# Twelve expert-layer blocks of 500 or 502 tokens in place of fourteen of 376 or 470, cut independently of the inverse transform's groups

## The chip, the cores and the metric

The kernel runs on one core of a Trainium2 chip. The metric is device time in microseconds (us); a lower time is better. Engines are called PE (TensorE), ACT (ScalarE), DVE (VectorE), POOL (GpSimd) and SP (SyncE, which issues the DMAs here).

## The reference

Three layers follow one another on 6016 tokens (2 sequences of 3008) of 256 channels:

```
X = rfft(x, axis=1)                      # float64 inside
Yr = Xr @ w_r - Xi @ w_i + b_r           # Yi likewise, with Xr @ w_i + Xi @ w_r + b_i
Y = soft_threshold(Y, 0.01)              # of real and imaginary part
x = irfft(Y, n=3008)
h = x @ w_in;  x = (h * cos(h)) @ w_out                    # first expert layer, 256 -> 2048 -> 256
h = x @ w_in2; out = (h * clip(h + 3, 0, 6) / 6) @ w_out2  # second expert layer
```

The weights of the expert layers come as float64. The kernel splits each operand of a product into a high and a low part of 12 significant bits, and a product is three matmuls (high by high, high by low, low by high).

## The kernel before, in words

**The transform.** The 3008 positions of a sequence are 64 interleaved rows of 47; two neighbouring rows make a pair, so there are 32 pairs a sequence and 94 tokens a pair. For each sequence a first stage (`a_part`, L322 to L337) takes the input in chunks of `A_CHUNKS` pairs: two of PE's float32 matmul instructions for each pair and each half of the channels into `zp`, then ACT copies the high part and DVE makes the low part. `load_x` fetches a chunk's table and input; `XB` chunks are loaded ahead, and each further one is issued after a chunk has been used. A second stage (`k2_step`, twelve a sequence) does the rest of the transform, the linear layer and the threshold in matmuls of 512 columns, and stores the result to DRAM (`u_dram`). The last products of the second stage of sequence 0 (`pend`) are done between the chunks of sequence 1's first stage.

**The inverse transform.** `load_u` (L270) reads a token block's `u_dram` back, and `y_part` (L278) makes one half of its channels with two PE instructions of 94 columns a pair. ACT and DVE split the result straight into the token tiles `tok`, of which a token set is handed out per block.

**The expert layers.** A sequence is cut into seven blocks of `BLOCK_PAIRS` = 5, 5, 5, 5, 4, 4, 4 pairs, that is, 470 or 376 tokens. A unit is one block by 128 of the 2048 hidden channels: six matmuls into a PSUM bank `h` (`mm_h`, L576), the nonlinearity on ACT and DVE (L587 to L611), the split into `gh` and `gl` (L619, L620), and, `DELAY` = 4 units later, six matmuls into two accumulators (`mm_out`, L633). The columns of each matmul are the tokens of the block, at most 512 of them. The order on PE, ACT and SP is written out by hand; DVE and POOL are ordered by the scheduler. The first layer runs `LEAD` blocks ahead of the second: first its blocks alone, then a unit of each layer in turn, and at the end blocks of the second layer alone. Four `h` banks are shared by all stages.

**The weights' conversion.** Float64 words become high and low parts in 32 chunks, 16 for each layer, in a fixed order. A chunk has five steps: clamp, shift, top, exponent, rest on DVE (L151 to L163), with a magnitude on ACT (L148) before and, after the rest, a sum on POOL (L164), the high part on ACT (L167) and the low part on POOL (L170). The high and low part of a chunk are emitted with the third and fourth step of the next chunk. Steps are spread over the program by `RATE_A` (one for each chunk of the first stage from `CV0` on), `RATE_W` (five for each two of the first ten steps of the second stage) and `RATE_M` (five for each four units). Before a product that needs a chunk, `require` emits what is still missing of it at once. `raw` holds the loaded words.

Of the kernel before, what the change touches and what calls it, by code (L numbers as in the profile page):

```python
# [19 lines left out]
# sequence 3008 = 47 * 64:  n = 64*n1 + n2,  k = k2 + 47*j,  n2 = 2*i + s  # L20
# [9 lines left out]
BLOCK_PAIRS = [5, 5, 5, 5, 4, 4, 4]  # L30
A_CHUNKS = [2] + [3] * 10
NFC = DFF // 128
LEAD = 4  # token blocks by which the first expert layer is ahead of the second
DELAY = 4  # units between a product with w_in and the product with w_out that takes it up
WARM = 9
IL, IM = 4, 1  # units after which the jobs of the first and of the later groups take turns
# steps of the weights' conversion in the unit's two places, in the transform, in the linear layer
# [3 lines left out]
LATE, CC, CV0 = [1, 4, 6], 7, 10  # L41
XB = 5
EG, PW = 0, 10
YP, YE = (0, 3, 6), (5, 2)


def _split(a):
    """float64 -> two float32 arrays of 12 significant bits each."""

    def rnd(v):  # L50
        b = v.astype(np.float32).view(np.uint32).astype(np.uint64)
        b = (b + 0x7FF + ((b >> 12) & 1)) & 0xFFFFF000
        return b.astype(np.uint32).view(np.float32)

    hi = rnd(a)
    return hi, rnd(a - hi.astype(np.float64))


def _trig(num, den):
    """cos, sin of 2*pi*num/den with exact zeros and ones."""  # L60
# [50 lines left out]
def fourier_moe_moe_kernel(ctx, tc, x, w_r, w_i, b_r, b_i, ta, tg, fg, win1, wout1, win2, wout2, out):  # L111
# [12 lines left out]
    # ---------------------------------------------------------------- weights  # L124
# [8 lines left out]
    def convert(src, dst_hi, dst_lo, name):  # L133
        """float64 words -> hi + lo, each of 12 significant bits; the instructions in stages"""
        raw = persist.tile([128, 512, 2], I32, tag="raw", bufs=3, name=f"raw{name}")
# [38 lines left out]
    class Converter:  # L174
        """Runs the conversions one VectorE instruction at a time, each chunk's end in the next one's course."""
# [71 lines left out]
    # ----------------------------------------------------------- token blocks  # L247
    blocks = []
    for b in range(NB):
        p0 = 0  # L250
        for n in BLOCK_PAIRS:
            blocks.append((b, p0, n))
            p0 += n
    NBLK = len(blocks)
    MAXP = max(BLOCK_PAIRS)
    MAXT = MAXP * TP

    def tok0(j):
        b, p0, n = blocks[j]
        return b * NSEQ + p0 * TP, n * TP  # L260
# [3 lines left out]
    # token blocks between the parts, transposed, as hi + lo: handed out and taken back in program order  # L264
# [3 lines left out]
    free_sets = [token_set(persist, i) for i in range(2)]  # L268

    def load_u(j):  # L270
        b, p0, n = blocks[j]
        ut = persist.tile([ROWS, MAXP, D], F32, tag="u_sb", name=f"u_sb{j}")
        sp.dma_start(ut[:, :n], u_dram[b][:, :, p0 : p0 + n, :].rearrange("s f i e -> (s f) i e"))
        tt = persist.tile([ROWS, MAXT], F32, tag="tg_sb", name=f"tg_sb{j}")
        sp.dma_start(tt[:, : n * TP], tg[:, p0 * TP : (p0 + n) * TP])
        u_sb[j], tg_sb[j] = ut, tt

    def y_part(j, ec):  # L278
        """inverse transform over k2 for one half of the channels of a token block"""
        b, p0, n = blocks[j]  # L280
        if ec == 0:
            y_sb[j] = free_sets.pop(0)
        yp = psum.tile([128, 512], F32, tag="h", bufs=4, name=f"yp{j}_{ec}")
        for i in range(n):
            pe.matmul(  # L285
                yp[:, i * TP : (i + 1) * TP],
                lhsT=u_sb[j][:, i, ec * 128 : (ec + 1) * 128],
                rhs=tg_sb[j][:, i * TP : (i + 1) * TP],
                start=True,
                stop=True,  # L290
            )
        yh, yl = y_sb[j][ec]
        t = n * TP
        act.activation(yh[:, :t], yp[:, :t], AF.Copy)
        dve.tensor_tensor(yl[:, :t], yp[:, :t], f32(yh[:, :t]), op=ALU.subtract)

    # -------------------------------------------------------------- attention
    with ExitStack() as actx:
        apool = actx.enter_context(tc.tile_pool(name="apool", bufs=1))
        with tc.manual_schedule(engines={mybir.EngineType.PE, mybir.EngineType.SP, mybir.EngineType.Activation}):  # L300
# [11 lines left out]
            def load_x(a):  # L312
# [3 lines left out]
                tt = apool.tile([ROWS, 3 * ROWS], F32, tag="ta", bufs=XB, name=f"ta{a}")  # L316
                sp.dma_start(tt[:, : n * ROWS], ta[:, p0 * ROWS : (p0 + n) * ROWS])  # L317
                xt = apool.tile([ROWS, 3, D], F32, tag="x", bufs=XB, name=f"x{a}")
# [22 lines left out]
            # dense products while the first loads are under way raise the tensor engine's clock  # L341
            warm = persist.tile([128, 2, D], BF16, tag="r", bufs=3, name="warm")
            dve.memset(warm, 0.0)
            # the sine's table is loaded before the data comes
# [61 lines left out]
            def b_mm(b, p):  # L406
                """minus the linear layer's output, for 2 k2"""
# [13 lines left out]
            def shrink_a(b, p):  # L421
                """minus the soft threshold, from u = -Y:  min(u + lam, relu(u - lam))"""
# [77 lines left out]
            for b in range(NB):  # L500
# [16 lines left out]
                for p in range(NP):  # L517
# [3 lines left out]
                    if b == NB - 1 and p in YP[1:3]:  # L521
                        y_part(0, YP[1:3].index(p))
                        if p == YP[2]:
                            load_u(1)
# [4 lines left out]
            y_part(1, 0)  # L529
            pend.pop(0)()  # L530
            y_part(1, 1)
            load_u(2)
# [3 lines left out]
    # ------------------------------------------------------------------- MoE  # L536
    mpool = ctx.enter_context(tc.tile_pool(name="mpool", bufs=1))
    with tc.manual_schedule(engines={mybir.EngineType.PE, mybir.EngineType.SP, mybir.EngineType.Activation}):
        free_sets += [token_set(mpool, i) for i in range(2, LEAD + 2)]
# [193 lines left out]
```

## Time and profile before

| what | us |
|---|---|
| runs: median of 3 (lowest, highest) | 1258.69 (1257.66, 1259.23) |
| the profiled execution: its span | 1257.1 |
| PE busy in it | 1247.8 |
| DVE busy | 845.4 |
| ACT busy | 813.2 |

The profiled execution's own time is given as its span, first to last instruction; the median of the runs is 1.6 us above it. A matmul's record ends when its result is out, and the next has begun long before, so a busy time close to the span says that PE had always something under way and not that it was at its peak. How long one matmul holds PE is read from the starts of consecutive ones.

### The profile page before, as it was taken

The page shows a single profiled execution, that of the slowest core. Times are in us where ns is not written, and L with a number is a line of the kernel's source. Part 1 is how long each engine was busy: PE and PEld are TensorE (multiplying, and loading weights), DVE is VectorE, ACT ScalarE, POOL GpSimd, SP SyncE. Part 2 cuts the span into 40 slices and gives each one's busy share as a digit, 9 for nine tenths or more (in the row PEclk, how much of TensorE's full clock was granted, in tenths as well). Part 3 has the DMA queues.
Part 4 walks back from the last instruction along what each step waited for, and adds up shares of the span by engine and source line. Part 5 has one row for each costly group of instructions (what it writes and reads, how often), then busy time and mean ns, then how long its engine had stood idle before and what let it go on. Part 6 is the DMA issues. An engine that isn't in the chain of part 4 may idle for free.

```text
span 1257.1 us, 17590 instructions
## 1 busy us (share of the span) xinstructions
PE 1247.8 (99%) x6401; PEld 1143.0 (91%) x6401; DVE 845.4 (67%) x1505; ACT 813.2 (65%) x1660; POOL 86.4 (7%) x68
## 2 busy tenths in 40 slices
PE   8999999999999999999999999999999999999998
PEld 7888888888899999999889999999999999999998
DVE  6887889999996655556556565665656556554444
ACT  5565679898876665656656666666656556654443
POOL 0212212222231000000000000000000000000000
PEclk7996999999999999999999999999999999999999
DMA  8265441122200100001000010000001000000000
GB/s 222 76 170 132 106 123 51 51 72 68 68 34 1 33 1 22 16 1 38 1 22 17 1 34 1 18 13 1 30 1 33 2 1 16 1 16 16 12 3 25
DMA packets 26599, 48.66 MB, mean 39 GB/s; under 512 B 2960, under 2 KB 16784, under 8 KB 26512
## 3 DMA queue, kind: packets, MB, share of 16 engines
q1 hardware_dynamic: 26512, 47.54, 13.0%
q8 instruction: 50, 0.82, 0.3%
q14 instruction: 37, 0.30, 0.1%
HBM read 35.08 MB, written 12.45 MB: 38 GB/s over the span
## 4 chain that ended last, share of the span: by engine, by line
PE 95%; DVE 2%; DMA 1%; ACT 1%; issue 1%; SPq 0%; DVEq 0%
PE acc L633 41%; PE h L576 41%; PE pp L390 6%; PE bp L413 3%; PE yp L285 2%; PE zp L326 2%; PE vp L444 1%; DMA x<-in_x_dram 1%; DVE zl L337 0%; DVE gl L620 0%; DVE r L588 0%; DVE h L609 0%; SPq L317 0%; ACT r L587 0%; SPq L319 0%
## 5 line engine op out<-in xcount | busy, mean ns | idle before, releaser
L611 DVE SCALAR_TENSOR_TENSOR h<-r,h 128x470 f32<-128x470 f32 (+1 forms) x224 | 136.7, 610 | 256.3 <-ACT r L592 256.3
L576 PE MATMUL h<-tok,w1i 128*128 128x470 f32 (+1 forms) x1344 | 300.3, 359 | 1.4 <-DVE gl L620 1.3
L576 PE MATMUL h<-tok,w2i 128*128 128x470 f32 (+1 forms) x1344 | 299.2, 358 | 0.0
L633 PE MATMUL acc<-gh,w2o 128*128 128x470 f32 (+1 forms) x896 | 284.1, 358 | 0.0
L633 PE MATMUL acc<-gh,w1o 128*128 128x470 f32 (+1 forms) x896 | 284.0, 358 | 0.0
L620 DVE TENSOR_TENSOR gl<-h,gh 128x376 fp32r<-128x376 f32 (+1 forms) x448 | 268.4, 599 | 0.5 <-ACT gh L619 0.5
L576 PEld LDWEIGHTS h<-tok,w1i 128*128 128x128 f32 x1344 | 244.2, 188 | 23.7 <-DVE gl L620 2.4
L576 PEld LDWEIGHTS h<-tok,w2i 128*128 128x128 f32 x1344 | 243.6, 188 | 16.9
L619 ACT ACTIVATE gh<-h 128x376 fp32r<-128x376 f32 (+1 forms) x448 | 236.0, 527 | 1.6 <-PE acc L633 0.5
L592 ACT ACTIVATE r<-h 128x470 f32<-128x470 f32 (+1 forms) x224 | 118.7, 530 | 178.1 <-PE h L576 178.0
L587 ACT ACTIVATE r<-h 128x470 int32<-128x470 f32 (+1 forms) x224 | 118.8, 530 | 135.7 <-PE h L576 135.1
L588 DVE SCALAR_TENSOR_TENSOR r<-r,h 128x470 f32<-128x470 int32 (+1 forms) x224 | 134.6, 601 | 95.1 <-ACT r L587 94.4
L633 PEld LDWEIGHTS acc<-gh,w2o 128*128 128x128 f32 x896 | 167.0, 188 | 13.2
L633 PEld LDWEIGHTS acc<-gh,w1o 128*128 128x128 f32 x896 | 167.0, 188 | 12.4
L633 PE MATMUL acc<-gl,w2o 128*128 128x470 f32 (+1 forms) x448 | 160.6, 358 | 0.0
L633 PE MATMUL acc<-gl,w1o 128*128 128x470 f32 (+1 forms) x448 | 159.9, 357 | 0.0
L600 ACT ACTIVATE r<-r 128x470 f32<-128x470 f32 (+1 forms) x224 | 126.3, 564 | 45.9 <-DVE r L588 45.9
L609 DVE TENSOR_TENSOR h<-r,h 128x470 f32<-128x470 f32 (+1 forms) x224 | 134.4, 600 | 0.0
L608 ACT ACTIVATE r<-r 128x470 f32<-128x470 f32 (+1 forms) x224 | 126.8, 566 | 0.0
L633 PEld LDWEIGHTS acc<-gl,w2o 128*128 128x128 f32 x448 | 84.3, 188 | 6.5
L633 PEld LDWEIGHTS acc<-gl,w1o 128*128 128x128 f32 x448 | 84.2, 188 | 6.2
L326 PEld LDWEIGHTS zp<-ta,x 96*128 96x128 f32 x256 | 42.6, 259 | 5.6 <-DVE zl L337 4.3
(79 smaller groups left out, 920.2 us busy)
## 6 DMA issues: line engine op xcount, KB each, us to landing
u_dram<-v SPq DMA_DIRECT2D x48, 128.0 KB, 2.4
x<-in_x_dram SPq DMA_DIRECT2D x20, 288.0 KB, 4.5
raw0i<-in_win_dram SPq DMA_DIRECT2D x8, 512.0 KB, 5.7
raw0o<-in_wout_dram SPq DMA_DIRECT2D x8, 512.0 KB, 3.8
raw1i<-in_win_dram SPq DMA_DIRECT2D x8, 512.0 KB, 3.2
raw1o<-in_wout_dram SPq DMA_DIRECT2D x8, 512.0 KB, 3.2
u_sb<-u_dram SPq DMA_DIRECT2D x8, 480.0 KB, 4.2
out_dram<-o SPq DMA_DIRECT2D x16, 235.0 KB, 2.2
```

Of the source, the lines that this page charges most:

```text
L390: pe.matmul(pp.rearrange("p a e -> p (a e)"), lhsT=za[:, kc, 2 * k2 : 2 * k2 + 2, :].rearrange("p r n -> p (r n)"), rhs=wb[:, kc, :], star ...
L576: pe.matmul(hp[:, :t], lhsT=w[:, c0 : c0 + 128], rhs=r[:, :t], start=(i == 0), stop=(i == 5))
L587: act.activation(k[:, :t], hp[:, :t], AF.Copy, bias=0.0, scale=1.0 / TWO_PI)
L588: dve.scalar_tensor_tensor(r[:, :t], k[:, :t], -TWO_PI, hp[:, :t], op0=ALU.mult, op1=ALU.add)
L592: act.activation(r[:, :t], hp[:, :t], AF.Relu, bias=3.0, scale=1.0)
L600: act.activation(mid[g][:, :t], mid[g][:, :t], AF.Abs)
L608: act.activation(r[:, :t], r[:, :t], AF.Sin, bias=math.pi / 2, scale=-1.0)
L609: dve.tensor_tensor(hp[:, :t], r[:, :t], hp[:, :t], op=ALU.mult)
L611: dve.scalar_tensor_tensor(hp[:, :t], r[:, :t], 6.0, hp[:, :t], op0=ALU.min, op1=ALU.mult)
L619: act.activation(gh[:, :t], hp[:, :t], AF.Copy)
L620: dve.tensor_tensor(gl[:, :t], hp[:, :t], f32(gh[:, :t]), op=ALU.subtract)
L633: pe.matmul(acc[n][d][:, :t], lhsT=w[:, fc % 2, d * 128 : (d + 1) * 128], rhs=r[:, :t], start=(fc == 0 and i == 0), stop=(fc == NFC - 1 an ...
```

## The change

The expert layers' blocks are cut by tokens and no more by pairs: twelve blocks, 502, 502, 500 four times. The inverse transform keeps groups of its own, 16 of four pairs (376 tokens); a group's result is written to one or two token blocks. Before a block of the first layer its groups are made, one or two of them. Three of the blocks (the fourth, seventh and tenth) need two groups. A group's load is issued behind the last product of the group before it. The lead falls from four blocks to three. The input comes in 8 chunks of four pairs a sequence, three loaded ahead; the token sets stay six, and `raw` goes from three buffers to two. Places in the first stage at which the late loads and the conversion begin are renumbered. Some comments are removed.

```
-BLOCK_PAIRS = [5, 5, 5, 5, 4, 4, 4]
-A_CHUNKS = [2] + [3] * 10
+YPAIRS = 4
+BLOCK_TOKENS = [502, 502, 500] * 4
+A_CHUNKS = [4] * 8
...
-LEAD = 4
-DELAY = 4
+LEAD = 3
+DELAY = 4
...
-LATE, CC, CV0 = [1, 4, 6], 7, 10
-XB = 5
+LATE, CC, CV0 = [1, 3, 4], 5, 7
+XB = 3
 EG, PW = 0, 10
-YP, YE = (0, 3, 6), (5, 2)
+YP = (0, 2, 4, 6, 8)
+YE = 3
...
-        raw = persist.tile([128, 512, 2], I32, tag="raw", bufs=3, name=f"raw{name}")
+        raw = persist.tile([128, 512, 2], I32, tag="raw", bufs=2, name=f"raw{name}")
...
+    NBLK = len(BLOCK_TOKENS)
+    MAXT = max(BLOCK_TOKENS)
+    starts = [sum(BLOCK_TOKENS[:j]) for j in range(NBLK + 1)]
+    YT = YPAIRS * TP
+    NG = NB * NPAIR // YPAIRS
...
+    def groups_of(j):
+        return range(-(-starts[j] // YT), -(-starts[j + 1] // YT))
...
-    free_sets = [token_set(persist, i) for i in range(2)]
+    free_sets = [token_set(persist, i) for i in range(3)]
...
+    def load_u(g):
+        if g >= NG:
+            return
+        b, p0 = divmod(g * YPAIRS, NPAIR)
+        ut = persist.tile([ROWS, YPAIRS, D], F32, tag="u_sb", name=f"u_sb{g}")
+        sp.dma_start(ut, u_dram[b][:, :, p0 : p0 + YPAIRS, :].rearrange("s f i e -> (s f) i e"))
+        tt = persist.tile([ROWS, YT], F32, tag="tg_sb", name=f"tg_sb{g}")
+        sp.dma_start(tt, tg[:, p0 * TP : (p0 + YPAIRS) * TP])
+        u_sb[g], tg_sb[g] = ut, tt
+
+    def y_part(g, ec):
+        yp = psum.tile([128, 512], F32, tag="h", bufs=4, name=f"yp{g}_{ec}")
+        for i in range(YPAIRS):
...
+        for j in range(NBLK):
+            t0, t1 = max(g * YT, starts[j]), min((g + 1) * YT, starts[j + 1])
+            if t0 < t1:
+                if j not in y_sb:
+                    y_sb[j] = free_sets.pop(0)
+                yh, yl = (z[:, t0 - starts[j] : t1 - starts[j]] for z in y_sb[j][ec])
+                src = yp[:, t0 - g * YT : t1 - g * YT]
+                act.activation(yh, src, AF.Copy)
+                dve.tensor_tensor(yl, src, f32(yh), op=ALU.subtract)
+        if ec == 1:
+            load_u(g + 1)
...
-                    if b == NB - 1 and p in YP[1:3]:
-                        y_part(0, YP[1:3].index(p))
-                        if p == YP[2]:
-                            load_u(1)
+                    if b == NB - 1 and p in YP[1:]:
+                        y_part(*divmod(YP[1:].index(p), 2))
...
-            y_part(1, 0)
+            y_part(2, 0)
             pend.pop(0)()
-            y_part(1, 1)
-            load_u(2)
+            y_part(2, 1)
...
-        free_sets += [token_set(mpool, i) for i in range(2, LEAD + 2)]
+        free_sets += [token_set(mpool, i) for i in range(3, LEAD + 3)]
...
-                jn = groups[i + 1][0][1]
-                if i > 0:
-                    events.setdefault(g0 + 1, []).append(lambda j=jn: load_u(j))
-                for e in range(2):
-                    events.setdefault(g0 + size - YE[e], []).append(lambda j=jn, e=e: y_part(j, e))
+                parts = [(g, e) for g in groups_of(groups[i + 1][0][1]) for e in range(2)]
+                for k, (g, e) in enumerate(reversed(parts)):
+                    events.setdefault(g0 + size - YE - 2 * k, []).append(lambda g=g, e=e: y_part(g, e))
```

The input's tiles `ta` and `x` grow from three pairs to four.

## Rows read from the trace of the kernel before

**Rows 1.** The page: PE's busy time, and its granted clock in 40 slices.

```profile
PE 1247.8 (99%) x6401; PEld 1143.0 (91%) x6401; DVE 845.4 (67%) x1505; ACT 813.2 (65%) x1660; POOL 86.4 (7%) x68
...
PEclk7996999999999999999999999999999999999999
```

**Rows 2.** The chain that ended last, shares of the span by engine and line.

```profile
PE 95%; DVE 2%; DMA 1%; ACT 1%; issue 1%; SPq 0%; DVEq 0%
```

**Rows 3.** Matmuls of the first layer by shape: count, busy us, mean ns.

```profile
L576 PE MATMUL h<-tok,w1i 128*128 128x470 f32 x768 | 185.3, 377 | 1.4 <-DVE gl L620 1.3
...
L576 PE MATMUL h<-tok,w1i 128*128 128x376 f32 x576 | 114.9, 335 | 0.0
```

**Rows 4.** PE in order of time, around 702 us: start us, us.

```profile
702.37 1.44 PE L576 MATMUL h<-tok,w1i 128*128 128x470 f32 x6
...
704.93 1.20 PE L576 MATMUL h<-tok,w2i 128*128 128x376 f32 x6
...
706.99 1.44 PE L576 MATMUL h<-tok,w1i 128*128 128x470 f32 x6
```

**Rows 5.** The chain in order of time, second stage of sequence 0: start us, us.

```profile
47.41 1.38 PE pp L390 x6
...
76.41 1.38 PE pp L390 x6
```

**Rows 6.** Weights' conversion of the second layer, by line: busy us, mean ns of one.

```profile
L170 POOL TENSOR_TENSOR w2i<-cva1i,w2i 128x512 fp32r<-128x512 f32 x8 | 11.4, 1424 | 38.5 <-ACT w2i L167 38.5
...
L164 POOL TENSOR_TENSOR cva1i<-cva1i,cvb1i 128x512 f32<-128x512 f32 x8 | 10.7, 1340 | 22.8 <-DVE cvb1i L163 22.8
...
L163 DVE SCALAR_TENSOR_TENSOR cvb1i<-raw1i,cvb1i 128x512 f32<-128x512 uint32 x8 | 5.5, 684 | 0.1
...
L148 ACT ACTIVATE cva1i<-raw1i 128x512 f32<-128x512 f32 x8 | 5.3, 666 | 0.0
...
L167 ACT ACTIVATE w2i<-cva1i 128x512 fp32r<-128x512 f32 x8 | 5.1, 633 | 0.0
```

**Rows 7.** PE, DVE and ACT in order of time, one unit of the alternating stage.

```profile
347.88 1.19 PE L576 MATMUL h<-tok,w1i 128*128 128x376 f32 x6
...
349.62 0.55 DVE L588 SCALAR_TENSOR_TENSOR r<-r,h 128x376 f32<-128x376 int32 x1
...
350.64 0.50 ACT L600 ACTIVATE r<-r 128x376 f32<-128x376 f32 x1
```

**Rows 8.** Stretches: length, busy us (x), granted clock, DMA share, GB/s.

```profile
16.80:30.40 13.60, 12.68 (x54) 12.17 (x55) 9.17 (x15) 6.68 (x11) 0.00 (x0) 0.50 0.79 224
84.60:95.30 10.70, 9.55 (x68) 8.37 (x67) 10.13 (x19) 8.43 (x17) 0.12 (x1) 1.00 0.67 194
95.30:111.10 15.80, 15.73 (x72) 15.23 (x71) 12.05 (x20) 9.61 (x16) 5.53 (x4) 0.50 0.91 237
...
188.00:342.00 154.00, 153.71 (x747) 136.16 (x746) 151.97 (x261) 137.45 (x274) 38.68 (x30) 1.00 0.18 61
```

**Rows 9.** The chain in order of time, first stage of sequence 0.

```profile
10.77 6.81 DMA x<-in_x_dram
17.72 10.52 PE zp L326 x48
```

**Rows 10.** DVE by shape: count, busy us, mean ns of one.

```profile
L620 DVE TENSOR_TENSOR gl<-h,gh 128x470 fp32r<-128x470 f32 x256 | 164.2, 641 | 0.0
L620 DVE TENSOR_TENSOR gl<-h,gh 128x376 fp32r<-128x376 f32 x192 | 104.2, 543 | 0.5 <-ACT gh L619 0.5
...
L337 DVE TENSOR_TENSOR zl<-zp,zh 128x288 fp32r<-128x288 f32 x40 | 30.3, 787 | 8.9 <-ACT zh L336 8.4
```

**Rows 11.** PE in order of time around a `y_part` of five pairs.

```profile
568.63 1.25 PE L285 MATMUL yp<-tg_sb,u_sb 96*128 96x94 f32 x10
569.66 0.68 PE L576 MATMUL h<-tok,w2i 128*128 128x470 f32 x2
```

**Rows 12.** Line 273, the loads of `u_sb`: from issue to landing.

```profile
DMA to landing us min/median/max: 3.6/4.1/9.8
```

More of the change, by code (lines that the diff above doesn't have):

```diff
@@ L245, in fourier_moe_moe_kernel @@
     cv = Converter()
[L248 to L256, printed above, removed]
+    NBLK = len(BLOCK_TOKENS)
[3 more added lines that the diff above has]
+    NG = NB * NPAIR // YPAIRS
     def tok0(j):
-        b, p0, n = blocks[j]
-        return b * NSEQ + p0 * TP, n * TP
+        return starts[j], BLOCK_TOKENS[j]
+    def groups_of(j):
+        return range(-(-starts[j] // YT), -(-starts[j + 1] // YT))
     u_sb, tg_sb, y_sb, x1_sb = {}, {}, {}, {}
@@ L266, in token_set @@
         return [[pool.tile([128, MAXT], F32R, name=f"tok{i}_{e}{z}") for z in range(2)] for e in range(2)]
-    free_sets = [token_set(persist, i) for i in range(2)]
[L270 to L284, printed above, removed]
+    free_sets = [token_set(persist, i) for i in range(3)]
[11 more added lines that the diff above has]
+        for i in range(YPAIRS):
             pe.matmul(
                 yp[:, i * TP : (i + 1) * TP],
-                lhsT=u_sb[j][:, i, ec * 128 : (ec + 1) * 128],
-                rhs=tg_sb[j][:, i * TP : (i + 1) * TP],
+                lhsT=u_sb[g][:, i, ec * 128 : (ec + 1) * 128],
+                rhs=tg_sb[g][:, i * TP : (i + 1) * TP],
                 start=True,
@@ L291, in y_part @@
             )
[L292 to L295, printed above, removed]
+        for j in range(NBLK):
[9 more added lines that the diff above has]
+            load_u(g + 1)
     with ExitStack() as actx:
@@ L315, in load_x @@
                 b, p0, n = a_list[a]
-                tt = apool.tile([ROWS, 3 * ROWS], F32, tag="ta", bufs=XB, name=f"ta{a}")
+                tt = apool.tile([ROWS, 4 * ROWS], F32, tag="ta", bufs=XB, name=f"ta{a}")
                 sp.dma_start(tt[:, : n * ROWS], ta[:, p0 * ROWS : (p0 + n) * ROWS])
-                xt = apool.tile([ROWS, 3, D], F32, tag="x", bufs=XB, name=f"x{a}")
+                xt = apool.tile([ROWS, 4, D], F32, tag="x", bufs=XB, name=f"x{a}")
                 sp.dma_start(xt[:, :n], x[b, :, p0 : p0 + n, :])
```

## The prediction

> **What bounds the kernel now.** I read the page first. PE is busy for 1247.8 of 1257.1 us, and its clock is granted in full (2.4 GHz) except near the start and near a tenth of the span [rows 1]. The chain that ended last lies on PE for 95% [rows 2]. So PE sets the time, and a change counts by what it does to the distance between PE's instructions, or by making PE wait.
>
> That distance can't be read from busy times: a matmul of 470 columns lasts 377 ns in its record [rows 3], but the next one starts much earlier. So I read the order in time. A unit is twelve matmuls. From the start of a 470-column unit at 702.37 to the next unit at 704.93 are 2.56 us, 213.3 ns for each matmul; from there to 706.99 the 376-column unit takes 2.06 us, 171.7 ns each [rows 4]. For 512 columns the second stage of the transform gives a price: from 47.41 to 76.41 are six steps of 21 matmuls (12 of L390, 6 of L413, 3 of L444), 29.00 us or 230.2 ns each [rows 5].
>
> **The matmuls of the expert layers.** 768 matmuls on line 576 make 128 units of 470 columns, and 576 make 96 of 376 [rows 3]; the second layer has as many. That is 256 x 2.56 + 192 x 2.06 = 655.4 + 395.5 = 1050.9 us. Afterwards there are 12 x 16 x 2 = 384 units, 4608 matmuls for 5376: 3072 of 502 columns and 1536 of 500. The columns streamed are the same, 6016 tokens x 2 x 192 = 2,310,144. What can be saved is only what 768 matmuls cost beyond their columns, and the three sizes don't agree on that. Between 470 and 512 a column costs (230.2 - 213.3) / 42 = 0.40 ns, which gives 226.2 ns at 502 and 225.4 at 500: 694.9 + 346.2 = 1041.1 us, a gain of **9.8**. The line through 376 and 470 rises 0.443 ns a column; it gives 227.5 and 226.6 ns, 1046.9 us, a gain of 4.0. If the price were proportional to columns at 470's rate (0.4538 ns) the sum would be 1048.4 us, a gain of 2.5. If a column took one cycle of the granted 2.4 GHz (0.4167 ns) and every matmul the 15.0 ns that 376 columns leave over, it would be 962.6 + 69.1 = 1031.7 us, a gain of 19.2. I take 9.8, since 502 lies between the two nearest sizes, and keep 2.5 and 19.2.
>
> A rule speaks against the change here. The Trainium skill ("TensorE: Matmul & The Clock Gate", section "Back-to-back issue gap") gives back-to-back matmuls N / 2.4 + 2.5 ns, so only 2.5 ns of each don't go with its columns. By that, 768 fewer would save 768 x 2.5 ns = 1.9 us (an estimate from that page). The trace disagrees on the size, 213.3 ns where the page would have 198.3 for 470 columns [rows 4], and doesn't say how much of the difference is fixed.
>
> **A wait for the second layer's weights.** The second layer's first unit comes after 48 units and no more after 64, and the conversion keeps its pace. Counted from the code: before, 12 steps in the first stages and 50 in the second, 62; now one chunk of sequence 0 and eight of sequence 1 give 9, with 50 makes 59. The 30th chunk (columns 1536 on of the second layer's w_in, lower half) is complete with step 4 x 1 + 5 x 30 = 154. It is wanted by unit 73 (48, one of the first layer, and two for each of twelve). By then 59 + 90 = 149 steps have been emitted, so `require` emits five at once. Before, that product was unit 89 and the conversion was finished by unit 75: no wait. Now the 30th chunk's rest (0.68 on DVE), sum (1.34 on POOL), high part (0.63 on ACT) and low part (1.42 on POOL) [rows 6] are 4.1 us in a row, with a magnitude of 0.67 on ACT between. Counted from the start T of the first-layer unit 72, PE comes to the fourth matmul of unit 73 at 2.71 + 0.68 = 3.4 us and to the sixth at 3.8. If rest and sum were done early (DVE's order is the scheduler's), ACT still passes L600 of unit 72 first, which in the trace ends 3.3 us after its unit's start [rows 7]; 0.67 + 0.63 + 1.42 later, the low part is there at T + 6.0, 2.1 us late. If rest runs where the program has it, after L588 (start T + 1.7 [rows 7]), two more vector operations and a step (0.55 + 0.6 + 0.6 + 0.4), it starts at about T + 3.9, and the low part is there at T + 8.0: 4.2 us late. I take **+3.0**. Behind the waiting matmul stand all of PE's work, and then ACT and DVE for lack of it. Nothing covers it. If PE's clock falls after it, it comes back late: near the start wide matmuls began at 28.24 [rows 9], the clock was at half up to 30.4 [rows 8] and full from 31.4 [rows 1], so up to 3.2 us at half speed, 1.6 us more.
>
> **First stage of sequence 1.** From 84.6 to 95.3 us DVE is busy 10.13 of 10.70 us; then the clock is at half (1.2 GHz) until after 111.1, and PE is full at that clock [rows 8]. An eviction of four pairs on DVE costs about 787 + 98 = 885 ns, by 787 for three [rows 10] and 98 ns for 94 more columns, 0.221 us a pair for 0.262: 2.6 us less over 64 halves of pairs, and three steps fewer. This matters while DVE is the limit; from 95.3 the half clock is. Against it: 12 pairs are loaded ahead and no more 14, a load is issued only two chunks before its use, and the DMAs are 91% busy there [rows 8]. I take **0**, from -5 (the clock stays up; DVE's 22.2 us [rows 8] less 2.6 and less 2 for steps then set the stage, 21 of 26.5 us with some idle) to +6 (half clock from the beginning: some 62 `zp` instructions at 10.52 / 48 = 0.22 us [rows 9] for half of that).
>
> **First stage of sequence 0.** PE waits here for input, and twelve pairs remain after the last wait [rows 9], as they will (three chunks of four for four of three). The first chunk has two pairs more, each 96 rows of 256 + 96 floats, 270 KB or 1.2 us at 224 GB/s [rows 8]; the warm-up matmuls cover part. I take **+0.3**, from 0 to +2.
>
> **Inverse transform.** The 256 PE instructions stay, 1.03 us for ten [rows 11]; there are four more parts, and 48 evictions on each of ACT and DVE for 28. On DVE one has a fixed part of 543 - 376 x (641 - 543) / 94 = 151 ns [rows 10], 3 us in all, under PE's work: DVE is idle a third of the span. Only where the first layer is alone is there no cover, 151.97 of 154.00 us [rows 8], but a wider block gives PE 6% more a unit and DVE's operations 33 ns (5%), and this stretch shrinks from 64 units to 48. I take **+0.5** for the parts, 0 to +1.5. Three blocks need two groups: the second group's load stands behind the first's last product, on SP behind a `raw` load that with two buffers now waits for its own chunk's rest, and has two units (5.4 us) to land; it takes 4.1 us [rows 12] and 0.7 to issue. **+0.5**, 0 to +4.
>
> **The end.** The last store has 500 columns for 376, about 0.13 us on ACT twice and some transfer: **+0.4**, 0 to 0.6. Fewer, longer operations on ACT and DVE lie beside PE and count nothing.
>
> **The sum.** -9.8 + 3.0 + 0 + 0.3 + 0.5 + 0.5 + 0.4 = -5.1 us on the span of 1257.1: 1252.0. The runs' median is 1.6 us above that span, so **1253.6 us**.
>
> **Rivals.**
> - *Columns are what costs.* The matmuls gain 2.5 us, as at 470's rate; the rest of the sum stays, and the change ends at 1257.1 - 2.5 + 4.7 + 1.6 = **1260.9**, slower. For it: 376 and 470 are nearly proportional (0.4566 and 0.4538 ns a column [rows 4]); against it: 512 costs 0.4496 [rows 5]. It decides when the gain is under 4.7 us, 6.1 ns for each of 768 matmuls. By the rule cited above, the Trainium skill's page "TensorE: Matmul & The Clock Gate" would end here too; the rows bear it out only as far as this rival's.
> - *The clock stays up in the second first stage.* -5 more: **1248.6**. For it: DVE's shorter work; against it: DVE was 95% busy when it fell [rows 8], and it still has the same tail of sequence 0 to do.
> - *A fixed 15 ns.* The gain is 19.2: **1244.2**.
> - *A clock at half for longer*, through sequence 1's first stage or after unit 73: +6, **1259.6**, no difference that can be told.
>
> **How the numbers follow.** A difference under 0.2% (2.5 us) can hardly be told from none. The forecast has 0.50, its own range 1248 to 1258 (0.43 of it faster, 0.07 the same). Columns have 0.22 (0.04 faster, 0.08 same, 0.10 slower), the clock that stays up and the fixed 15 ns 0.13 together (faster), the longer half clock 0.15 (0.03, 0.08, 0.04). Faster 0.63, same 0.23, slower 0.14. Leaving out one in ten at either end, beyond the fixed 15 ns and beyond columns, gives **1244 to 1262**.
>
> **What will show it.** A 502-column unit should take 2.71 us from start to start; 2.68 would be the fixed cost, 2.735 columns alone. A gap of 2 to 4 us should stand on PE in the fourth block's turn with the second layer's first (unit 73, about 70 us after that turn begins), released by POOL's L170. The granted clock from 85 to 116 us should look as before. The prediction is wrong if units differ from 2.71 by over 0.02 us, or if PE shows other gaps over 1 us in the expert layers, at the second groups' loads above all.

## The result: a little slower, 1265.1 us where 1253.6 was forecast

The changed kernel took 1265.12 us, the median of 6 runs (1263.34 to 1271.82); the kernel before took 1259.68 us beside it (1257.66 to 1261.42). The ratio is 1.0052 [1.0029, 1.0075]. The profiled execution took 1263.34 us with a span of 1261.6 us, 4.5 us more than the span of before; the forecast was 5.1 us less.

The page of the changed kernel: PE's busy time and instructions, the granted clock in 40 slices, and the chain's shares.

```profile
PE 1241.5 (98%) x5633; PEld 1035.5 (82%) x5633; DVE 827.2 (66%) x1349; ACT 791.6 (63%) x1468; POOL 85.4 (7%) x68
...
PEclk7997999999998999999999999999999999999999
...
PE 94%; DVE 2%; ACT 1%; DMA 1%; issue 1%; POOL 0%; SPq 0%; DVEq 0%; POOLq 0%; ACTq 0%
```

Beside [rows 1] PE is busy for 6.3 us less, in 768 instructions fewer, and yet the span is longer: PE waited more. The clock's row says where to look. Its 13th digit is 8, and that slice (378 to 410 us) had full clock before. The chain now names POOL, which it did not before [rows 2].

Three marks of PE's timeline divide each execution: the first product of the expert layers, the last one, and the end. Before, they are at 174.43, 1253.40 and 1257.09 us; after, at 173.70, 1257.52 and 1261.57. So the transform is 0.73 us shorter, the expert layers go from 1078.97 to **1083.81** us, and the tail from 3.69 to 4.05. The whole loss is in the expert layers.

First what a product costs there. PE in order of time, a stretch with no waits (start us, us; a unit runs from one line of L578 to the next, with six matmuls of L635 between):

```profile
701.98 1.53 PE L578 MATMUL h<-tok,w2i 128*128 128x502 f32 x6
...
710.17 1.51 PE L578 MATMUL h<-tok,w1i 128*128 128x502 f32 x6
...
1059.58 1.52 PE L578 MATMUL h<-tok,w2i 128*128 128x500 f32 x6
...
1064.98 1.52 PE L578 MATMUL h<-tok,w2i 128*128 128x500 f32 x6
```

From 701.98 to 710.17 are three units, 2.73 us each; about a quarter of those of 502 columns take 2.71. Two units of 500 take 5.40 us, 2.70 each. That is 256 x 2.725 + 128 x 2.70 = 1043.2 us, 7.7 less than the 1050.9 of before; 9.8 were forecast. Averaged over all units that have no inverse-transform part in them and lie within 0.045 us of their size's median, a unit takes 2.726 (502 columns) and 2.705 us (500), and before 2.560 (470) and 2.057 (376): 1044.2 for 1050.2. So the gain is **6 to 8** us, and 7.7 stands below for the units that are shown.

Then the wait. PE around unit 73, the first to need columns 1536 on of the second layer's `w_in` (in brackets the idle time before it and what ended it):

```profile
372.01 1.52 PE L578 MATMUL h<-tok,w2i 128*128 128x502 f32 x6
...
374.72 1.52 PE L578 MATMUL h<-tok,w1i 128*128 128x502 f32 x6
...
378.98 0.72 PE L578 MATMUL h<-tok,w2i 128*128 128x502 f32 x2 [1.38 <-ACT w2i L169]
380.87 0.50 PE L578 MATMUL h<-tok,w2i 128*128 128x502 f32 x1 [1.16 <-POOL w2i L172]
384.74 1.21 PE L578 MATMUL h<-tok,w2i 128*128 128x502 f32 x2 [3.37 <-ACT w2i L169]
386.29 0.79 PE L578 MATMUL h<-tok,w2i 128*128 128x502 f32 x1 [0.34 <-POOL w2i L172]
...
389.39 1.81 PE L578 MATMUL h<-tok,w1i 128*128 128x502 f32 x6
```

A unit here takes 2.71 us (372.01 to 374.72). The next two take 4.26 and 10.41, and the two behind them 0.30 and 0.27 more than their like: **9.8 us** lost, where the forecast had 3.0. The idle times in brackets add up to 6.25 us; most of the rest is the clock's, as shown below. There are four waits, not two, one pair for the chunk of `w_in`'s first 128 rows and one for the second. ACT and POOL show them as one chain in series:

```profile
378.29 0.63 ACT L169 ACTIVATE w2i<-cva1i 128x512 fp32r<-128x512 f32 x1
...
384.06 0.63 ACT L169 ACTIVATE w2i<-cva1i 128x512 fp32r<-128x512 f32 x1 [2.55 <-POOL cva1i L166]
...
379.07 1.74 POOL L172 TENSOR_TENSOR w2i<-cva1i,w2i 128x512 fp32r<-128x512 f32 x1 [4.19 <-ACT w2i L169]
382.71 1.31 POOL L166 TENSOR_TENSOR cva1i<-cva1i,cvb1i 128x512 f32<-128x512 f32 x1 [1.90 <-DVE cvb1i L165]
384.76 1.47 POOL L172 TENSOR_TENSOR w2i<-cva1i,w2i 128x512 fp32r<-128x512 f32 x1 [0.74 <-ACT w2i L169]
```

The first chunk's high part (378.29) and low part (379.07) are followed by the whole of the second chunk and not only its end: its five steps on DVE (378.08 to 382.56), sum (382.71), high part (384.06), low part (384.76). PE's clock fell behind it. The stretch, with its length, busy us (x) of PE, PEld, DVE, ACT and POOL, granted clock, DMA share and GB/s:

```profile
383.20:390.00 6.80, 4.92 (x11) 3.52 (x12) 5.67 (x8) 2.78 (x5) 3.58 (x3) 0.50 0.28 80
```

The clock is at half (1.2 GHz) for these 6.80 us, and full on either side.

Last, two gaps that before does not have, each behind a `y_part` where the first layer runs alone:

```profile
245.15 1.52 PE L578 MATMUL h<-tok,w1i 128*128 128x502 f32 x6
...
247.88 1.03 PE L285 MATMUL yp<-tg_sb,u_sb 96*128 96x94 f32 x8
249.73 1.62 PE L578 MATMUL h<-tok,w1i 128*128 128x502 f32 x6 [0.82 <-DVE gl L622]
```

This period is 4.58 us where other units with such a part take 3.52; the period at 280.57 is 4.60. Together they cost 2.2 us.

The theory at this point: the expert layers gain 7.7 us by their products, lose 9.8 at unit 73 because more of the conversion is owed at that unit (more of its steps are not yet emitted) than I had counted, and lose some 2.5 at the parts and the second groups. Its rivals: the shorter lead is not at fault but the input by four pairs, which shifts the whole conversion; and the products' gain comes from the width as such (a multiple, a rounding, an address), not from columns and count.

### The profile page after: what moved, and what is told of

The parts are those of the page before. It is cut to its first block, busy times and chain, and to the rows that moved or that the text cites. A ratio compares the mean times of both kernels' runs of the same rounds, so it can differ in the third digit from the quotient of the medians.

```text
span 1261.6 us, 15535 instructions
## 1 busy us (share of the span) xinstructions
PE 1241.5 (98%) x5633; PEld 1035.5 (82%) x5633; DVE 827.2 (66%) x1349; ACT 791.6 (63%) x1468; POOL 85.4 (7%) x68
## 4 chain that ended last, share of the span: by engine, by line
PE 94%; DVE 2%; ACT 1%; DMA 1%; issue 1%; POOL 0%; SPq 0%; DVEq 0%; POOLq 0%; ACTq 0%
PE h L578 41%; PE acc L635 41%; PE pp L397 5%; PE bp L420 2%; PE zp L333 2%; PE yp L285 2%; PE vp L451 1%; DMA x<-in_x_dram 1%; DVE zl L344 1%; DVE gl L622 0%; POOL w2i L172 0%; ACT r L589 0%; DVE u L435 0%; ACT r L602 0%; SPq L324 0%
## 5 line engine op out<-in xcount | busy, mean ns | idle before, releaser
L613 DVE SCALAR_TENSOR_TENSOR h<-r,h 128x502 f32<-128x502 f32 (+1 forms) x192 | 131.4, 684 | 261.4 <-ACT r L594 261.3
L578 PE MATMUL h<-tok,w2i 128*128 128x502 f32 (+1 forms) x1152 | 293.7, 389 | 6.3 <-ACT w2i L169 4.8
L578 PE MATMUL h<-tok,w1i 128*128 128x502 f32 (+1 forms) x1152 | 294.4, 391 | 3.5 <-DVE gl L622 3.3
L635 PE MATMUL acc<-gh,w1o 128*128 128x502 f32 (+1 forms) x768 | 267.8, 389 | 0.0
L635 PE MATMUL acc<-gh,w2o 128*128 128x502 f32 (+1 forms) x768 | 267.8, 390 | 0.0
L578 PEld LDWEIGHTS h<-tok,w2i 128*128 128x128 f32 x1152 | 217.2, 189 | 52.3 <-ACT w2i L169 5.5
L622 DVE TENSOR_TENSOR gl<-h,gh 128x502 fp32r<-128x502 f32 (+1 forms) x384 | 258.7, 674 | 0.7 <-ACT gh L621 0.7
L578 PEld LDWEIGHTS h<-tok,w1i 128*128 128x128 f32 x1152 | 214.9, 188 | 46.4 <-DVE gl L622 4.6
L621 ACT ACTIVATE gh<-h 128x502 fp32r<-128x502 f32 (+1 forms) x384 | 225.2, 586 | 1.2 <-PE acc L635 1.0
L590 DVE SCALAR_TENSOR_TENSOR r<-r,h 128x502 f32<-128x502 int32 (+1 forms) x192 | 129.9, 677 | 117.0 <-ACT r L589 116.3
L635 PEld LDWEIGHTS acc<-gh,w2o 128*128 128x128 f32 x768 | 145.0, 189 | 28.9
L635 PEld LDWEIGHTS acc<-gh,w1o 128*128 128x128 f32 x768 | 144.5, 188 | 29.3
L635 PE MATMUL acc<-gl,w2o 128*128 128x502 f32 (+1 forms) x384 | 149.9, 390 | 0.0
L635 PE MATMUL acc<-gl,w1o 128*128 128x502 f32 (+1 forms) x384 | 149.7, 390 | 0.0
L602 ACT ACTIVATE r<-r 128x502 f32<-128x502 f32 (+1 forms) x192 | 120.1, 625 | 41.1 <-DVE r L590 41.1
L610 ACT ACTIVATE r<-r 128x502 f32<-128x502 f32 (+1 forms) x192 | 120.3, 627 | 0.0
L635 PEld LDWEIGHTS acc<-gl,w2o 128*128 128x128 f32 x384 | 72.5, 189 | 15.4
L635 PEld LDWEIGHTS acc<-gl,w1o 128*128 128x128 f32 x384 | 72.1, 188 | 15.6
```

The source lines that it names most:

```text
L578: pe.matmul(hp[:, :t], lhsT=w[:, c0 : c0 + 128], rhs=r[:, :t], start=(i == 0), stop=(i == 5))
L590: dve.scalar_tensor_tensor(r[:, :t], k[:, :t], -TWO_PI, hp[:, :t], op0=ALU.mult, op1=ALU.add)
L602: act.activation(mid[g][:, :t], mid[g][:, :t], AF.Abs)
L610: act.activation(r[:, :t], r[:, :t], AF.Sin, bias=math.pi / 2, scale=-1.0)
L613: dve.scalar_tensor_tensor(hp[:, :t], r[:, :t], 6.0, hp[:, :t], op0=ALU.min, op1=ALU.mult)
L621: act.activation(gh[:, :t], hp[:, :t], AF.Copy)
```

## Experiments

All ratios are to the kernel before, run on the same chip (its medians there: 1258.17 us for e1 to e4, 1258.34 for e5 to e8, 1258.23 for e9 to e12; the table has the last).

| run | median us (range) | ratio | first expert product, us | expert layers, us |
|---|---|---|---|---|
| before | 1258.23 (1255.77 to 1263.22) | 1 | 174.4 | 1078.97 |
| e1_pace | 1257.51 (1255.78 to 1260.74) | 0.9988 [0.9975, 1.0000] | 176.6 | 1073.86 |
| e2_lead3 | 1267.57 (1264.53 to 1269.01) | 1.0055 [1.0034, 1.0076] | 176.2 | 1084.87 |
| e3_chunks4 | 1260.87 (1259.66 to 1265.79) | 1.0019 [1.0005, 1.0032] | 174.7 | 1079.42 |
| e4_504 | 1265.41 (1262.99 to 1269.16) | 1.0045 [1.0029, 1.0061] | 176.8 | 1082.79 |
| e5_512 | 1257.62 (1254.20 to 1261.23) | 0.9993 [0.9980, 1.0006] | 181.1 | 1074.55 |
| e6_480 | 1258.44 (1255.56 to 1262.95) | 1.0001 [0.9989, 1.0014] | 175.0 | 1075.35 |
| e7_slow | 1259.77 (1254.03 to 1261.64) | 1.0005 [0.9990, 1.0019] | 178.4 | 1075.02 |
| e8_chunks3 | 1257.04 (1254.86 to 1260.71) | 0.9991 [0.9980, 1.0003] | 176.5 | 1074.40 |
| e9_five | 1270.87 (1269.98 to 1276.59) | 1.0094 [1.0077, 1.0112] | 180.3 | 1090.43 |
| e10_none | 1257.11 (1254.21 to 1260.17) | 0.9986 [0.9973, 0.9998] | 179.0 | 1073.71 |
| e11_pad | 1259.89 (1255.04 to 1261.24) | 0.9996 [0.9981, 1.0010] | 181.1 | 1074.27 |
| e12_before12 | 1258.81 (1257.17 to 1263.39) | 1.0007 [0.9993, 1.0022] | 172.8 | 1078.93 |

The last two columns are of the one profiled execution. The first expert product comes anywhere from 172.8 to 181.1 us, about as wide as the spread of a kernel's runs; where the code up to there is the same (e1_pace, e7_slow, e10_none) it comes at 176.6, 178.4 and 179.0. The time of the expert layers is much steadier, so it is what I compare. What lies ahead of them is taken up again further down.

### Is the wait at unit 73 what was lost? (e1_pace)

```
-EG, PW = 0, 10
+EG, PW = 0, 12
...
-                    cv.step(RATE_M[4 + g % 4])
+                    cv.step(g % 2 if g >= 48 else RATE_M[4 + g % 4])
```

> The changed kernel with the weights' conversion ahead of its use: two more steps of the second stage take part (PW 12), and from unit 48 on a step more in every second unit, so that nothing is owed at unit 73. Theory L (the late conversion is the loss): the gap of some 10 us around 380 us is gone, the time falls by 9 to 11 us to about 1255 and so below the kernel before by 3 to 6 us. Rival C (columns are what costs, the wider blocks gain nothing): the time falls by less than 4 us, to 1261 or more. Rival I (the input by four pairs costs): no change beyond 2 us.

The gap at unit 73 is gone, the clock stays full from 115.6 us on, and the expert layers take 1073.86 us, 9.95 less than after. The median is only 7.6 us lower (1257.51 for 1265.12), under theory L's 9 to 11: in the profiles the first expert product comes 2.9 us later than in after. The two gaps behind `y_part` stay (0.82 us ahead of 252.58 and 0.87 ahead of 288.03). But two things were changed here, the debt and the pace; e10_none separates them.

### Which part of the change brings it? (e2_lead3, e3_chunks4, e8_chunks3)

Of the kernel before with the lead alone:

```
-LEAD = 4  # token blocks by which the first expert layer is ahead of the second
+LEAD = 3  # token blocks by which the first expert layer is ahead of the second
```

> The kernel before with the lead of three blocks alone, fourteen blocks kept. Counted from the code, the conversion then owes six steps at unit 73 (58 + 90 = 148 of 154). Theory L: a gap of 4 to 8 us on PE at unit 73, about 1264 to 1268 us. Rivals C and I: no such gap, 1259 to 1261 us.

Of the kernel before with the input by four pairs alone:

```
-A_CHUNKS = [2] + [3] * 10
+A_CHUNKS = [4] * 8
...
-LATE, CC, CV0 = [1, 4, 6], 7, 10
-XB = 5
+LATE, CC, CV0 = [1, 3, 4], 5, 7
+XB = 3
```

> The kernel before with the input by four pairs alone (eight chunks a sequence, three ahead). Theory L: within 2 us of before, 1258 to 1262; the first stage of sequence 0 ends about 1 us later, that of sequence 1 up to 2 us earlier. Rival I: 1264 us or more.

Of e1_pace with the old chunks of the input:

```
-A_CHUNKS = [4] * 8
+A_CHUNKS = [2] + [3] * 10
...
-LATE, CC, CV0 = [1, 3, 4], 5, 7
-XB = 3
+LATE, CC, CV0 = [1, 4, 6], 7, 10
+XB = 4
```

> As e1_pace, but with the input in chunks of two and three pairs as before, four chunks ahead, and the late loads and the conversion's start where they were. If the input by four pairs costs what e3_chunks4 showed, the time falls by 2 to 3 us, to about 1255; otherwise it stays within 1 us of e1_pace.

The lead alone makes the old blocks slower by 0.55%, and PE waits at the same place:

```profile
362.60 1.44 PE L576 MATMUL h<-tok,w1i 128*128 128x470 f32 x6
...
365.66 0.69 PE L576 MATMUL h<-tok,w2i 128*128 128x470 f32 x2 [0.35 <-ACT w2i L167]
367.74 0.48 PE L576 MATMUL h<-tok,w2i 128*128 128x470 f32 x1 [1.38 <-POOL w2i L170]
368.94 0.70 PE L576 MATMUL h<-tok,w2i 128*128 128x470 f32 x2 [0.72 <-ACT w2i L167]
370.48 0.76 PE L576 MATMUL h<-tok,w2i 128*128 128x470 f32 x1 [0.84 <-POOL w2i L170]
...
373.38 0.90 PE L576 MATMUL h<-tok,w1i 128*128 128x470 f32 x3
```

Two units that take 2.56 us elsewhere take 3.06 and 7.72, 5.7 us lost. Here six steps are owed (below), since the old chunks leave the conversion three steps further on. The input by four pairs adds 0.45 us to the expert layers and 0.25 to what lies ahead of them; by its ratio it costs 0.05 to 0.32%. In the expert layers it brings a gap of 0.70 us behind a `y_part`, ahead of 245.83, which before does not have (its rows are in the last section). Taking it out of e1_pace changes the time by nothing that can be told (0.9991 for 0.9988). So its share is small and its sign stays open; the lead brings the wait.

### How the wait grows with the steps owed (e9_five, e10_none, e12_before12)

A count in program order, with each call of the conversion as the code has it, gives 55 steps at the expert layers' start and nine owed at unit 73, not 59 and five: in `k2_step` the step of `RATE_W[0]` stands under `if p >= 2`, so a second stage emits 23 steps and not 25. With `PW` at 11 five are owed, the prediction's own case; with 12 none.

```
-EG, PW = 0, 10
+EG, PW = 0, 11     (e9_five)
+EG, PW = 0, 12     (e10_none; e12_before12 is the same edit of the kernel before)
```

> After's kernel with PW 11 for 10: two steps more in each second stage, 59 by the expert layers' start, so that 59 + 90 = 149 of 154 steps are emitted by unit 73. That is the prediction's own count of five owed (one chunk's end), where after itself has nine (two chunks' ends in a row). Theory A (the count was wrong, the price was right): the units 72 and 73 take 3 us more than two plain units, 2.1 to 4.2, with at most 1.6 us for the clock, and the run is 5 to 7 us faster than after, 1258 to 1260. Theory B (the price was wrong too: each chunk's end passes ACT and POOL behind other work, and the clock falls after any wait of some us): 5 us or more are lost there, the granted clock is half for some us behind it, and the run is 1260 to 1262.

> After's kernel with PW 12 for 10: five steps more in each second stage, 65 by the expert layers' start, so that none is owed at unit 73; the pace in the expert layers stays as it is (the first experiment changed that as well). Theory A (the owed steps are the whole loss at unit 73): units 72 and 73 are plain, 5.4 us together, the clock stays full, first product to last sum takes 1083.8 - 9.8 = 1074.0 us, and the run is 1255 to 1258, as the first experiment. Theory B (the steadier pace in the alternating part did a share of the first experiment's gain): a gap of 1 us or more stays at or near unit 73, and the run is 1259 or more.

> The kernel before with PW 12 for 10 alone: the conversion five steps further on at each second stage's end, blocks, lead and input as before. It is the control for the runs with PW 12. Theory A (PW 12 gains only where a step was owed; before owes none): no difference, 1258.2 within 1.5. Theory B (PW 12 gains by itself, in the second stages or by ending the conversion sooner): 2 us or more faster, below 1256.5, and then the gain of the wider blocks in the first experiment is smaller by that.

With none owed (e10_none), units 72 to 74 are plain, and the expert layers take 1073.71 us, 10.1 less than after; the pace did nothing in e1_pace. In the kernel before, which owes none, the same edit changes nothing (1078.93 for 1078.97).

With five owed (e9_five), one pair of waits is left:

```profile
396.50 0.84 PE L578 MATMUL h<-tok,w2i 128*128 128x502 f32 x3
398.42 0.72 PE L578 MATMUL h<-tok,w2i 128*128 128x502 f32 x2 [1.08 <-ACT w2i L169]
399.95 0.50 PE L578 MATMUL h<-tok,w2i 128*128 128x502 f32 x1 [0.81 <-POOL w2i L172]
...
402.18 2.55 PE L578 MATMUL h<-tok,w1i 128*128 128x502 f32 x6
...
405.95 1.52 PE L578 MATMUL h<-tok,w2i 128*128 128x502 f32 x6
```

Unit 73 takes 5.68 us (2.97 more), the next 3.77 (1.06 more, at half clock: its six products last 2.55 us). So, with the half clock behind the wait counted in, 4.0 us for five, 5.7 for six (of 470 columns), 9.8 for nine, none for none.

And yet this run was the slowest of all, by a place where neither theory had looked. PE at 304 us, and then SP's queue and DVE there:

```profile
301.65 1.52 PE L578 MATMUL h<-tok,w1i 128*128 128x500 f32 x6
...
313.27 1.99 PE L285 MATMUL yp<-tg_sb,u_sb 96*128 96x94 f32 x8 [8.75 <-DMA tg_sb<-in_tg_dram]
314.97 2.85 PE L578 MATMUL h<-tok,w1i 128*128 128x500 f32 x6
319.65 1.52 PE L578 MATMUL h<-tok,w1i 128*128 128x500 f32 x6
```

```profile
307.25 0.35 SPq L145 DMA_DIRECT2D raw1i<-in_win_dram  x1
307.69 0.38 SPq L276 DMA_DIRECT2D u_sb<-u_dram  x1
308.12 0.42 SPq L278 DMA_DIRECT2D tg_sb<-in_tg_dram  x1
...
305.59 1.59 DVE L165 SCALAR_TENSOR_TENSOR cvb1o<-raw1o,cvb1o 128x512 f32<-128x512 uint32 x1
```

The loads of the next group stand on SP behind a `raw` load, and with two `raw` buffers that load goes out only when the chunk two back has done its rest (L165, ending at 307.18). The loads then take 5 us to land, and PE waits 8.75 us with nothing to do. The unit takes 13.32 us and the one behind it 4.68, where e10_none has 3.51 and 2.79 at the same unit: 11.7 us. In after, the same two queue entries stand the other way round:

```profile
304.34 0.31 SPq L276 DMA_DIRECT2D u_sb<-u_dram  x1
...
308.88 11.07 SPq L145 DMA_DIRECT2D raw1i<-in_win_dram  x2
```

Four steps more of the conversion moved a `raw` load past a group's loads on a queue that takes its entries in order. There the group's load goes out 4.5 us ahead of the `raw` load, and nothing in the code keeps that order.

### What sets the price of a product (e4_504, e5_512, e6_480, e11_pad)

```
-BLOCK_TOKENS = [502, 502, 500] * 4
+BLOCK_TOKENS = [504, 504, 496] * 4     (e4_504, an edit of after)
+BLOCK_TOKENS = [512] * 11 + [384]      (e5_512, an edit of e1_pace)
+BLOCK_TOKENS = [480] * 12 + [256]      (e6_480, an edit of e1_pace)
...
-    MAXT = max(BLOCK_TOKENS)
+    MAXT = 512                         (e11_pad, an edit of e1_pace)
```

> The changed kernel with blocks of 504, 504, 496 tokens. The 502-column unit takes 2.73 us and the 500-column unit 2.70. If a column count that is no multiple of four costs extra, the 504-column unit takes 2.71 to 2.72 and the 496-column unit 2.67 to 2.68, and the time falls by 3 to 5 us. If the price is in proportion to columns (Rival C), they take 2.74 and 2.69, and the time stays within 1 us of the changed kernel. The gap at unit 73 stays.

> Changed kernel with the conversion ahead (as e1_pace) and blocks of 512 tokens eleven times and 384 once. Units so far: 376 columns 2.05 us, 470 2.55, 496 and 500 2.70, 502 and 504 2.71 to 2.73. Theory S (a matmul costs as many columns as the next multiple of 32, at 0.4167 ns, and 11 to 14 ns on top): a 512-column unit takes 2.70 to 2.74 and the 384-column unit 2.05 to 2.07, the expert layers' matmuls fall by some 16 us against e1_pace, to a time of about 1241. Theory C (in proportion to columns): 2.78 and 2.09 us, 1253 to 1259.

> As e5_512, with thirteen blocks, 480 tokens twelve times and 256 once. Theory S: a 480-column unit takes 2.55 us like one of 470, a 256-column unit 1.42; the matmuls sum to 1025 us where e1_pace has 1043, and the time is about 1240. Theory C: 2.61 and 1.39 us, 1047 us, 1258 to 1262.

> The first experiment's kernel (no step owed) with token tiles of 512 columns for 502 (MAXT), the blocks as they are: the same instructions on the same columns, each tile at another address. Theory A (the matmuls of 500 and 502 columns lie 1 to 2 ns under the line through the other sizes because of where their columns lie in the tile): units of 502 columns go from 2.71 to 2.73 us to 2.74, the line's price, and the time goes up by some 3 us, 1260 to 1261. Theory B (it is the count of columns, or nothing that the address decides): units stay at 2.71 to 2.73 and 2.70, the time at 1257.5 within 1.5.

Starts of units in order of time, first e5_512:

```profile
700.63 1.55 PE L578 MATMUL h<-tok,w1i 128*128 128x512 f32 x6
...
708.99 1.55 PE L578 MATMUL h<-tok,w2i 128*128 128x512 f32 x6
...
1241.23 1.21 PE L578 MATMUL h<-tok,w2i 128*128 128x384 f32 x6
...
1249.58 1.21 PE L578 MATMUL h<-tok,w2i 128*128 128x384 f32 x6
```

then e6_480:

```profile
700.46 1.47 PE L578 MATMUL h<-tok,w1i 128*128 128x480 f32 x6
...
710.89 1.47 PE L578 MATMUL h<-tok,w1i 128*128 128x480 f32 x6
...
1236.31 0.87 PE L578 MATMUL h<-tok,w2i 128*128 128x256 f32 x6
...
1246.16 0.86 PE L578 MATMUL h<-tok,w2i 128*128 128x256 f32 x6
```

Three units of 512 take 8.36 us, 232.2 ns for each matmul; four of 384 take 8.35 (174.0), four of 480 take 10.43 (217.3), seven of 256 take 9.85 (117.3). A line through 256 and 512 rises 0.449 ns a column and leaves **2.4 ns** over. It gives 174.8 at 384, 217.8 at 480, and for the kernel before 213.3 at 470 and 171.2 at 376, where 213.3 and 171.7 were read [rows 4]. So the fixed part of a matmul here is small, 2.4 ns by this line, and 768 matmuls fewer are worth 768 x 2.4 = 1.8 us. It is not known to the nanosecond: units of 376 columns alone take 2.05 us at the end of before and 2.08 at the end of e2_lead3, 171.1 and 173.3 ns. The rule that the prediction cites (the Trainium skill, "TensorE: Matmul & The Clock Gate", section "Back-to-back issue gap") has 2.5 ns for this part: with that these runs agree, and only its price of a column is lower than the 0.449 ns here. The section calls that formula the gap of an isolated matmul, and for a stream of weight loads and matmuls it gives 131 ns at 512 columns, where 232.2 were read here.

The sizes of the change lie below the line: 500 has 225.0 ns for 226.8, 502 has 225.8 to 227.5 for 227.7. Of the other 6 of the 7.7 us some 4.7 come from there, and 1.2 from 376 columns, read 0.5 ns above the line. Three ideas about the sizes fell. That a matmul costs the next multiple of 32 columns (Theory S of e5_512 and e6_480) would make units of 512 and 480 columns take 2.70 to 2.74 and 2.55 us; they take 2.79 and 2.61. With 504 and 496, multiples of four and eight, units take 2.71 to 2.74 and 2.70 us, and e4_504 is as slow as after, with the same wait at 382 us. With tiles of 512 columns (e11_pad), units of 502 stay at 2.71 and 2.73, those of 500 at 2.71, and the expert layers at 1074.27 us: the address moves a unit by 0.02 us at most and the sum by 0.4. (Its median, 1259.89 us, is close to the first theory's, but in its profile what it has over e1_pace lies ahead of the expert layers, whose first product comes at 181.1 us for 176.6.) The time of the expert layers lies within 1.7 us for 480, 502 and 512 (1073.7 to 1075.4 us), once the wait is gone.

### Do the gaps behind `y_part` come from the conversion? (e7_slow)

Of e1_pace, four steps for each four units in place of five while the first layer is alone, and behind it two for each unit in place of three for each two:

```
-                    cv.step(g % 2 if g >= 48 else RATE_M[4 + g % 4])
+                    cv.step(1 if g >= 48 else 0)
```

> As e1_pace, but the conversion takes four steps per four units while the first layer runs alone (five in e1_pace) and two per unit from unit 48 on. If the two gaps of 1.1 us behind an inverse transform's product (252 and 287 us in e1_pace) come of DVE having no idle time there, they vanish and the time falls by about 2 us. If they come of the four h banks, they stay.

One gap is gone, the other falls to 0.47 us (ahead of 288.45), and new ones of 0.25 and 0.90 us stand ahead of 348.73 and 383.23, in the alternating part. The expert layers take 1075.02 us for 1073.86: what one place gains the others lose. So the conversion's place in time decides where the gaps stand (the last section shows by which step); a pace that has none was not found.

## Why the prediction was wrong, step by step

**The wait for the second layer's weights** is the step that failed: "12 steps in the first stages and 50 in the second, 62; now ... 59", and "`require` emits five at once". The second stages emit 46, so that 55 + 90 = 145 of 154 steps are there at unit 73, and nine are owed. Nine are the 30th chunk's five steps, of which the forecast had only the last, and four behind them, with the 29th chunk's high and low part among them: two chunks' ends run one behind the other through DVE, POOL and ACT. The place, the product and the releaser were as forecast, and so was the price of five: +3.0 with up to 1.6 for the clock was said, 4.0 with the clock was measured in e9_five. With nine it cost 9.8 in place of 3.0. That is 6.8 of the 9.6 us by which the span was missed (the median was missed by 11.5; the profiled run was the fastest of its six), and it alone turns the sign: e10_none, with none owed, is at 0.9986 [0.9973, 0.9998].

**The matmuls** were sized at -9.8 and measured -7.7 by the units shown, -6.0 over all units. The rise of 0.40 ns a column came from setting the transform's mixed steps (230.2 ns at 512) against the expert layers' units (213.3 at 470); 512 columns in the expert layers cost 232.2. Of the rivals, *columns are what costs* was right in the mechanism (a fixed part of 2.4 ns, not 15), and 500 and 502 are cheaper than that for a reason that stays open.

**Inverse transform and second groups' loads**, +0.5 and +0.5. With none owed the expert layers gain 5.3 us, 6.0 to 7.7 by the products less 0.7 to 2.4 for all else. So the two terms had about the right size, but by luck: what stands there are the two gaps behind `y_part`, 2.2 us that were not foreseen, and after has no wait over 0.5 us for a group's load. The bound that I gave for a group's load that stands behind a `raw` load, 0 to +4, was too tight: e9_five paid 11.7, the clock included. The mechanism was the one described.

**First stage of sequence 1** went from 27.23 us to 25.74 in the two profiles, but in the experiments it takes 24.6 to 27.7 with the old chunks and 27.1 to 28.3 with those of four pairs, so the shorter time of that one profile is no gain by the change; whether 0 should have been a loss stays open. A four-pair eviction on DVE takes 1012 ns, not 885, so most of the 2.6 us that I saw in it were not there.

**First stage of sequence 0** took 1.2 us longer for +0.3 forecast, and **the end** +0.36 for +0.4. The transform as a whole was 0.7 us shorter in this profile, less than profiles with the same code up to there differ in.

**Ahead of the expert layers** the sum had 0.3 us, and there something is lost that no run explains. e10_none's expert layers are 5.3 us shorter than those of before and its end is 0.4 longer, and yet by its ratio it is only 1.8 us faster [0.3 to 3.4]. In the four profiles with the old chunks of the input the first expert product comes at 172.8 to 176.5 us, in the ten with chunks of four pairs at 173.7 to 181.1. But e8_chunks3, with the old chunks, is no faster than e1_pace. The two `raw` buffers and the two more `y_part`s in the transform were not tried alone.

**The half clock for longer** came true behind unit 73 only: 0.50 from 383.2 to 390.0 us, inside the 9.8 above.

## What to carry to other kernels

When a schedule owes work at a fixed point, count the steps by running the emitting code's conditions, not by its rates; four steps missed here turned 3 us into 10. The price of such a debt is the length of the chain that it leaves (here two chunks' ends in series), and PE's clock can fall on top. And a pace, once changed, must be looked at on every in-order queue that it feeds: the mend that owed less was slower than none at all, because it put a waiting load ahead of one that PE needed.

## What the runs showed of the hardware

**DVE's conversion steps take 1 us more when they start beside a POOL operation.** In after the operation ahead of the first gap behind a `y_part` is one of them:

```profile
246.82 1.68 DVE L165 SCALAR_TENSOR_TENSOR cvb1i<-raw1i,cvb1i 128x512 f32<-128x512 uint32 x1
...
249.01 0.67 DVE L622 TENSOR_TENSOR gl<-h,gh 128x502 fp32r<-128x502 f32 x1
...
246.66 1.30 POOL L172 TENSOR_TENSOR w2i<-cva1i,w2i 128x512 fp32r<-128x512 f32 x1 [7.68 <-ACT w2i L169]
```

L165 takes 0.68 us elsewhere. It starts 0.16 us after POOL's L172 and ends 0.54 us after it, as if it had begun when POOL ended. All eight conversion steps of after that last over 1 us overlap a POOL operation so, and three of them (379.72, 382.94 and 385.14) lie in unit 73's wait, the first of them in the chain that PE waits for. L590 and the products' other operations, which read PSUM, are not lengthened (L590 takes 678 ns without a POOL operation beside it and 679 with one). The Trainium skill ("SBUF — State Buffer", section "Who interferes with whom") says that a DVE operation with two inputs in SBUF, as L165 is, contends with a POOL operation that reads SBUF, by a shared port pair that is an exclusive lock; the rows of L165 and L172 agree. Such a step goes with the gaps behind `y_part`. Above, it holds up L622, which ends at 249.68, and PE goes on at 249.73. Before has sixteen such steps and no gap there, but none of them stands at a part. e3_chunks4, with the blocks of before and the conversion three steps behind, has one there:

```profile
242.98 1.69 DVE L163 SCALAR_TENSOR_TENSOR cvb1i<-raw1i,cvb1i 128x512 f32<-128x512 uint32 x1
...
245.83 1.54 PE L576 MATMUL h<-tok,w1i 128*128 128x470 f32 x6 [0.70 <-DVE gl L620]
```

Over the fourteen profiles, all 16 parts from 240 to 400 us with a conversion step of over 1 us that starts in the 3 us ahead of them, or beside them, have a gap of 0.35 to 0.94 us behind them; the other 83 have 0.20 at most, but for one of 0.36. The two go together in every profile, but that is no experiment: no run took POOL out.

**The clock at the start falls at different times in the same code.** In after it is half from 14.6 us and the first stage ends at 29.0; in e10_none, with the same code up to there, it is half from 8.1 us and the stage ends at 31.4. The rows are windows of after first, then of e10_none:

```profile
14.60:29.00 14.40, 13.78 (x63) 13.60 (x64) 8.95 (x13) 6.65 (x9) 0.00 (x0) 0.50 0.86 226
```

```profile
5.20:8.10 2.90, 2.19 (x18) 2.05 (x19) 0.95 (x1) 1.74 (x2) 0.00 (x0) 1.00 0.83 232
8.10:31.40 23.30, 23.30 (x111) 23.30 (x111) 14.86 (x19) 11.78 (x16) 0.00 (x0) 0.50 0.72 207
```

At the early fall PE had been busy for 2.19 of 2.90 us, waiting for input. What decides between the two starts was not tried.
